# Retention attention and a Strassen MLP on one core: values, last chunk, scores and sums of neighbouring pairs in one run of small tiles, the last block written by quarters on two queues, and one weight piece finished by halves

## The chip, the cores and the metric

The kernel runs on one core of one Trainium2 chip. The metric is the device time of one execution in microseconds (us); times of runs are medians. Nearly all executions here agree within 0.3%, so a change of 0.7% can be seen but a change of 0.1% can not, except inside a trace, where the same stretch repeats within a few hundredths of a microsecond from trace to trace. The granted clock is the share of TensorE's full speed that the chip allowed. All runs on record are of the fast state, with a mean granted clock of 0.995 or more.

## The reference, cut to what matters

```python
# attention, causal with decay: batch 8, heads 8, length 576, head dimension 64
scores = (q @ k.transpose(0, 1, 3, 2)) / 8
Dmat[h, i, j] = gamma[h] ** (i - j) if i >= j else 0
attn = (scores * Dmat) @ v
x = attn.transpose(0, 2, 1, 3).reshape(4608, 512)
# MLP: 4608 tokens, 512 -> 2048 -> 512, PReLU in between
h = x @ w_in
g = max(h, 0) + alpha * min(h, 0)
out = g @ w_out
```

The kernel works the attention in chunks of 64 positions (nine a head): scores inside a chunk, running sums of k-times-v between chunks, and values from both. It takes two heads (a pair) at a time. The MLP runs by blocks of 256 tokens, each in 8 units; from the third block on, a unit is one level of a seven-product Strassen scheme, with weights and inputs combined beforehand. Per unit TensorE computes `ph` (seven products for h), VectorE makes g and its combinations, and TensorE computes `po` (seven products for out).

## The kernel before

In the loop, units of blocks already finished hide the attention of the next batch row. One pair had two separate visits ("excursions") to small array tiles: the scores and sums inside a unit, between its ph and the po of the unit ahead, and the values two units later.

```python
    def mlp_unit(kb, i, front=None):
        ...                                   # 14 matmuls into ph[0], ph[1], 128x128 tiles
        rest = front(ph[0][:, 3]) if front else None   # scores and sums, 64x64 tiles
        ...                                   # ScalarE and VectorE: g from ph
        combine(3, ins)                       # GpSimd: three weight combinations, while some wait
        if rest:
            rest()                            # VectorE: masks of the scores
        pend.append((kb, i, g))
        if len(pend) > 1:
            mlp_out()                         # po of the unit before
...
    def pair_values(n, vn, mt):
        ...
        pv = [ps_tile([P, (j1, NJ - j1)[i], C], f"pv{i}_{n}") for i in range(2)]
        for j in range(NJ):
            for h2 in range(2):               # 128x64 tiles
                nc.tensor.matmul(pv[j >= j1][half(h2), j - (j1 if j >= j1 else 0)],
                                 vn[:, h2, j], mt[:, h2, j], start=True, stop=True)
        ...                                   # ScalarE copies pv into xb, the MLP's input
...
        for u in range(nq):
            front = None
            if u in begin:
                ...
                front = pair_front(n, *turned.pop(n), loaded[n][0], loaded[n][3])
            pop_units(1, front)
            if u - 1 in begin:
                later.pop(0)()                # VectorE: running sums
            if u - 2 in begin:
                n = begin[u - 2]
                if n + 1 < len(pairs):
                    scale_pair(n + 1)         # GpSimd scales q
                    turned[n + 1] = transposes(n + 1)   # VectorE turns k and q
                pair_values(n, loaded[n][3], mts.pop(n))
                del loaded[n]
```

At the end of a block `out_block` adds the products on VectorE, and both halves (128 tokens of 512 values, 256 KB each) leave by SyncE's queue. At the start, `piece_out` turns a raw piece of w_in into the form that TensorE reads: three steps on VectorE, one on GpSimd.

## Time and profile before

| | before |
|---|---|
| time, median (three runs) | 1019.35 us (1018.71 to 1019.44) |
| span in the trace | 1018.5 us |
| TensorE (PE) / VectorE (DVE) / ScalarE (ACT) / GpSimd (POOL) busy | 98 / 76 / 26 / 18% |
| first Strassen unit begins | 153.95 us |
| from there to the ninth unit's start | 57.06 us |
| ninth unit's start to the last unit's start (119 units, 22 pairs) | 793.02 us |
| last matmul's end to the end of the span | 5.11 us |

The last four rows are read from the timeline of PE: a unit begins with the first record of its ph group. They cut the span into the parts that the change touches. The page's fourth part gives the shares of the chain that ended last, that is, of the work followed back from the last instruction, at each step to what released it; in the kernel before:

```profile
PE 94%; DVE 3%; DMA 1%; ACT 0%; issue 0%; SPq 0%; POOL 0%; DVEq 0%; ACTq 0%
```

The 3% of DVE are the one long stretch in which PE is not the chain; it lies in the loop's first 50 us.

### The profile page before, as it was taken

To read this page: it belongs to the slowest core of one execution; us is meant where nothing else is said; L and a number is where in the kernel's file an instruction comes from. 1 tells how busy PE (TensorE), PEld (TensorE's weight loads), DVE (VectorE), ACT (ScalarE), POOL (GpSimd) and SP (SyncE) were. 2 spreads that over 40 slices of the span, in tenths; PEclk is the share of its full clock that TensorE was granted. 3 is DMA by queue.
4 is the path that set the end of the run, shared out by engine and by line. 5 is a ranking of instruction groups with operands and counts; after the bars stand their busy time and mean duration, and the time that the engine had idled before them with its cause. 6 is when DMAs were issued, how large, how long until landed. Compare 5 with 4: busy or idle time off the path is not lost.

```text
span 1018.5 us, 23084 instructions
## 1 busy us (share of the span) xinstructions
PE 1001.3 (98%) x9385; PEld 894.2 (88%) x9385; DVE 778.3 (76%) x2086; ACT 269.4 (26%) x605; POOL 179.2 (18%) x201
## 2 busy tenths in 40 slices
PE   6999999999999999999999999999999999999997
PEld 5666668899999999999999999999999999999997
DVE  6669966878887888768778788887878777667665
ACT  4556653223222222122021312232222211000000
POOL 5656674300100020100010000200020001010000
PEclk8999999999999999999999999999999999999999
DMA  9975744322231323112112313222313000000000
GB/s 238 238 194 140 185 74 103 60 60 48 52 64 40 63 37 69 25 45 48 44 25 56 60 45 60 57 48 54 62 45 60 13 23 1 22 1 21 2 21 22
DMA packets 229308, 64.30 MB, mean 63 GB/s; under 512 B 214337, under 2 KB 222545, under 8 KB 229201
## 3 DMA queue, kind: packets, MB, share of 16 engines
q1 hardware_dynamic: 227088, 62.29, 27.1%
q8 instruction: 74, 1.21, 0.5%
q10 hardware_dynamic: 2112, 0.53, 0.3%
q14 instruction: 34, 0.27, 0.1%
HBM read 53.35 MB, written 9.44 MB: 62 GB/s over the span
## 4 chain that ended last, share of the span: by engine, by line
PE 94%; DVE 3%; DMA 1%; ACT 0%; issue 0%; SPq 0%; POOL 0%; DVEq 0%; ACTq 0%
PE ph L463 38%; PE po L381 37%; PE ph L419 6%; PE po L398 6%; PE pv L656 3%; PE ps L614 1%; PE ps L620 1%; DMA w_out<-in_k_dram 1%; PE ph L614 1%; DVE su L589 0%; DVE g L476 0%; PE pt L697 0%; DVE mt L636 0%; PE ps L716 0%; PE ps L556 0%
## 5 line engine op out<-in xcount | busy, mean ns | idle before, releaser
L381 PE MATMUL po<-w_out,g 128*128 128x256 f32 x1792 | 410.9, 381 | 0.2
L381 PEld LDWEIGHTS po<-w_out,g 128*128 128x128 f32 x1792 | 330.1, 190 | 42.7 <-DVE g L487 1.3
L476 DVE TENSOR_TENSOR g<-ph,g 128x256 f32<-128x256 f32 (+1 forms) x512 | 187.0, 386 | 127.2 <-ACT g L471 75.2
L463 PE MATMUL ph<-xb,w_in 128*128 128x128 f32 x2048 | 272.7, 276 | 0.0
L463 PEld LDWEIGHTS ph<-xb,w_in 128*128 128x128 f32 x2048 | 257.1, 192 | 7.9 <-issue 0.7
L463 PE MATMUL ph<-xt,w_in 128*128 128x128 f32 x1536 | 213.8, 275 | 0.7 <-DVE g L476 0.7
L463 PEld LDWEIGHTS ph<-xt,w_in 128*128 128x128 f32 x1536 | 192.2, 192 | 1.1 <-PE ph L463 0.8
L487 DVE TENSOR_TENSOR g<-g 128x128 f32<-128x128 f32 x512 | 127.2, 289 | 5.4
L471 ACT COPY g<-ph 128x128 f32<-128x128 f32 x128 | 34.1, 266 | 327.7 <-PE ph L463 217.1
L528 POOL TENSOR_TENSOR qx<-qx,tabx 128x576 f32<-128x576 f32 x28 | 32.3, 1153 | 379.6 <-DMA qx<-in_q_dram 223.4
L481 DVE SCALAR_TENSOR_TENSOR g<-g 128x512 f32<-128x512 f32 x128 | 91.3, 714 | 3.8
L479 DVE TENSOR_SCALAR g<-g,alpha 128x256 f32<-128x256 f32 x256 | 84.3, 370 | 2.8
L597 ACT COPY vn<-su 64x512 f32<-64x512 f32 x56 | 34.6, 617 | 135.2 <-DVE su L591 134.5
L419 PE MATMUL ph<-xb,w_in 128*128 128x256 f32 x256 | 61.7, 397 | 0.8 <-POOL w_in L314 0.8
L419 PEld LDWEIGHTS ph<-xb,w_in 128*128 128x128 f32 x256 | 50.1, 198 | 11.0 <-issue 2.4
L398 PE MATMUL po<-w_out,g 128*128 128x512 f32 x128 | 58.6, 599 | 0.9 <-DVE g L435 0.9
L625 DVE SCALAR_TENSOR_TENSOR mt<-ph,th,mask 64x64 f32<-64x64 f32 x48 | 13.6, 283 | 52.5 <-PE ph L614 52.2
L665 ACT COPY xb<-pv 128x256 f32<-128x256 f32 (+3 forms) x84 | 22.7, 321 | 109.8 <-PE pv L656 109.8
L636 DVE SCALAR_TENSOR_TENSOR mt<-ps,th,mask 64x256 f32<-64x256 f32 x96 | 46.1, 481 | 2.3
L533 ACT ACTIVATE vn<-vn,tabv 64x576 f32<-64x576 f32 x56 | 43.3, 774 | 8.7 <-DMA vn<-in_v_dram 7.8
L398 PEld LDWEIGHTS po<-w_out,g 128*128 128x128 f32 x128 | 23.4, 190 | 24.5 <-issue 22.9
L589 DVE SCALAR_TENSOR_TENSOR su<-su,gch 128x64 f32<-128x64 f32 x84 | 43.1, 513 | 2.1
(134 smaller groups left out, 717.0 us busy)
## 6 DMA issues: line engine op xcount, KB each, us to landing
out_dram<-osb SPq DMA_DIRECT2D x36, 256.0 KB, 2.3
kx<-in_k_dram SPq DMA_DIRECT2D x112, 72.0 KB, 2.6
qx<-in_q_dram SPq DMA_DIRECT2D x112, 72.0 KB, 3.0
vn<-in_v_dram SPq DMA_DIRECT2D x56, 144.0 KB, 3.2
kn<-in_k_dram SPq DMA_DIRECT2D x56, 144.0 KB, 3.3
raw<-in_moe_w_in_dram SPq DMA_DIRECT2D x24, 256.0 KB, 4.5
raw<-in_moe_w_out_dram SPq DMA_DIRECT2D x10, 512.0 KB, 5.4
w_in<-in_moe_w_out_dram SPq DMA_DIRECT2D x6, 512.0 KB, 5.7
```

Source lines behind the costliest of these rows:

```text
L381: nc.tensor.matmul(acc[kb][n // 2][:, n % 2, :], g[:, x, :], w_out[i][:, y, :], start=(i == 0 and n % 2 == 0), stop=(i == NU - 1 and (n % ...
L398: nc.tensor.matmul(acc[kb][m], g[:, 2 * x + m], w_out[i][:, 2 * x:2 * x + 2].rearrange("p x f -> p (x f)"), start=(i == 0 and x == 0), sto ...
L419: nc.tensor.matmul(ph[:, x], w_in[i // UST][:, cc // 2 * 2 + x, i % UST, cc % 2], xb[kb][:, cc], start=(cc == 0 and x == 0), stop=(cc == N ...
L463: nc.tensor.matmul(ph[m][:, o], w_in[i // UST][:, l, i % UST, cc], r[:, cc], start=(n in (0, 3) and cc == 0), stop=(n in (2, 6) and cc == ...
L476: nc.vector.tensor_tensor(out=o, in0=x0, in1=x1, op=ALU.add)
L479: nc.vector.tensor_scalar(g[:, 4 + 2 * m:6 + 2 * m], g[:, 2 * m:2 * m + 2], 0.0, alpha[:, fc:fc + 1], ALU.min, ALU.mult)
L481: nc.vector.scalar_tensor_tensor(out=g[:, 0:4].rearrange("p x t -> p (x t)"), in0=g[:, 0:4].rearrange("p x t -> p (x t)"), scalar=0.0, in1 ...
L487: ins = nc.vector.tensor_tensor(out=g[:, o, :], in0=g[:, x0, :], in1=g[:, x1, :], op=op)
L533: nc.scalar.activation(vn[x, h2], vn[x, h2], ACTF.Copy, scale=tabv[x, c:c + 1])
L589: nc.vector.scalar_tensor_tensor(out=su[:, j], in0=su[:, j - 2], scalar=g2, in1=su[:, j], op0=ALU.mult, op1=ALU.add)
L597: nc.scalar.copy(vn[half(h2), h2, 1:], su[half(h2)])
L636: nc.vector.scalar_tensor_tensor(out=mt[to, h2, p2:NJ - 1:2], in0=ps[p2][half(x), 0], scalar=th[to, 3, h:h + 1], in1=mask[to, None, :].to_ ...
```

## The change

The intent is to enter and leave the small tiles once a pair instead of twice: after the po of one unit come the values of pair n-1, then the last chunk's scores of pair n, then its other scores and sums, then the next unit's ph. The values now use the two ph banks, which are empty at that moment, and the last chunk's scores take the free corner of the second. Apart from that, the last block leaves in four quarters on two queues, and the second piece of w_in is finished in halves. The diff, cut to its core:

```diff
@@ piece_out
+            for f in (slice(0, P), slice(P, HM)) if at == 1 else (slice(0, HM),):
+                dst_e, c_e, a_e, hi_e, lo_e = [y[:, :, f] for y in (dst, c, a, hi, lo)]
                 ...                          # the same three VectorE steps and GpSimd step
@@ out_block
+        if kb == NKB - 1:
+            for (m, x), eng in (((0, 0), nc.sync), ((1, 1), nc.scalar), ((0, 1), nc.sync),
+                                ((1, 0), nc.scalar)):
+                t0 = kb * TB + m * P
+                eng.dma_start(out[t0:t0 + P, x * HM:(x + 1) * HM], osb[:, m, x])
+            return
@@ mlp_unit
-        rest = front(ph[0][:, 3]) if front else None
-        if rest:
-            rest()
@@ the loop
+    def joint(n):
+        pv = [ps_h.tile([P, 8, C], FP32, tag=f"psh{m}", name=f"pv{m}_{n}") for m in range(2)]
+        extra = pv[1][:, 7]
+        def last_chunk():
+            if n < len(pairs):
+                kT, qT = turned[n]
+                for h2 in range(2):
+                    nc.tensor.matmul(extra[half(1 - h2)], kT[half(h2), chunk(NJ - 1)],
+                                     qT[half(h2), chunk(NJ - 1)], start=True, stop=True)
+        if n - 1 in mts:
+            pair_values(n - 1, loaded.pop(n - 1)[3], mts.pop(n - 1), pv, last_chunk)
+        else:
+            last_chunk()
+        if n == len(pairs):
+            return
+        pair_front(n, *turned.pop(n), loaded[n][0], loaded[n][3], extra)
+        ...                                   # load_pair(n + 1), operands(n + 1) later
-        (positions of pairs and the loop shown above)
+        at = [u + (u % NU == 0) for u in (c * nq // NPAIR + 2 for c in range(NPAIR))]
+        if b == 2:
+            at = [0, 3] + at[1:]
+        for u in range(nq):
+            first = queue[0][1] == 0
+            pop_units(1)
+            if later and not first:
+                later.pop(0)()
+            if u in at:
+                joint(n)
+                n += 1
```

More of the change, by code (lines that the diff above doesn't have):

```diff
@@ L306, in piece_out @@
             c = ps_h.tile([P, 2, HM], INT32, tag="psh1", name=f"wc_{at}")
-            nc.vector.tensor_scalar(c.bitcast(FP32), a, HI_MIN, HI_MAX, ALU.max, ALU.min)
-            nc.vector.tensor_scalar(c, c, 3, 0x3FFFFFF8,
-                                    ALU.logical_shift_left, ALU.bitwise_and)
-            nc.vector.scalar_tensor_tensor(out=dst.bitcast(INT32), in0=hi, scalar=-0x40000000,
-                                           in1=c, op0=ALU.bitwise_and, op1=ALU.bitwise_or)
-            nc.gpsimd.tensor_tensor(out=dst.bitcast(INT32), in0=dst.bitcast(INT32), in1=lo,
-                                    op=ALU.add)
+            for f in (slice(0, P), slice(P, HM)) if at == 1 else (slice(0, HM),):
+                dst_e, c_e, a_e, hi_e, lo_e = [y[:, :, f] for y in (dst, c, a, hi, lo)]
+                nc.vector.tensor_scalar(c_e.bitcast(FP32), a_e, HI_MIN, HI_MAX, ALU.max, ALU.min)
+                nc.vector.tensor_scalar(c_e, c_e, 3, 0x3FFFFFF8,
+                                        ALU.logical_shift_left, ALU.bitwise_and)
+                nc.vector.scalar_tensor_tensor(out=dst_e.bitcast(INT32), in0=hi_e,
+                                               scalar=-0x40000000, in1=c_e,
+                                               op0=ALU.bitwise_and, op1=ALU.bitwise_or)
+                nc.gpsimd.tensor_tensor(out=dst_e.bitcast(INT32), in0=dst_e.bitcast(INT32),
+                                        in1=lo_e, op=ALU.add)
             free.append(t)
@@ L449, in combine_x, with mlp_unit @@
             nc.gpsimd.tensor_tensor(out=o, in0=x0, in1=x1, op=ALU.subtract)
-    def mlp_unit(kb, i, front=None):
+    def mlp_unit(kb, i):
         if kb not in xt:
@@ L508, in enqueue, with pop_units @@
                 queue.extend((kb, i) for i in range(NU))
-    def pop_units(n, front=None):
+    def pop_units(n):
         for _ in range(min(n, len(queue))):
             kb, i = queue.pop(0)
-            mlp_unit(kb, i, front)
+            mlp_unit(kb, i)
             if i == NU // 2 and kb + 1 < NKB and ready[kb + 1] <= done[0]:
@@ L601, with pair_front @@
     later = []
-    def pair_front(n, kT, qT, kn, vn):
+    def pair_front(n, kT, qT, kn, vn, extra):
         c = pairs[n][1]
@@ L607, in pair_front @@
         assert C == D and NJ == 9
-        def products(extra):
-            ps = [ps_tile([P, 2, NM - 1, C], f"ps{p2}_{n}") for p2 in range(2)]
-            for j in (NJ - 1, *range(NJ - 1)):
-                for h2 in range(2):
-                    x = half((1 - h2, h2)[j % 2])
-                    nc.tensor.matmul(extra[x, 0:C] if j == NJ - 1 else ps[j % 2][x, 0, j // 2],
-                                     kT[half(h2), chunk(j)], qT[half(h2), chunk(j)],
-                                     start=True, stop=True, skip_group_check=True)
-            for j in range(NJ - 1):
-                for h2 in range(2):
-                    x = half((h2, 1 - h2)[j % 2])
-                    nc.tensor.matmul(ps[j % 2][x, 1, j // 2], kn[half(1 - h2), j],
-                                     vn[half(1 - h2), h2, j], start=True, stop=True,
-                                     skip_group_check=True)
-            for h2 in range(2):
-                to = half(1 - h2)
+        ps = [ps_tile([P, 2, NM - 1, C], f"ps{p2}_{n}") for p2 in range(2)]
@@ new lines, in pair_front @@
+        for j in range(NJ - 1):
+            for h2 in range(2):
+                x = half((1 - h2, h2)[j % 2])
+                nc.tensor.matmul(ps[j % 2][x, 0, j // 2],
+                                 kT[half(h2), chunk(j)], qT[half(h2), chunk(j)],
+                                 start=True, stop=True, skip_group_check=True)
+        for j in range(NJ - 1):
+            for h2 in range(2):
+                x = half((h2, 1 - h2)[j % 2])
+                nc.tensor.matmul(ps[j % 2][x, 1, j // 2], kn[half(1 - h2), j],
+                                 vn[half(1 - h2), h2, j], start=True, stop=True,
+                                 skip_group_check=True)
@@ new lines, in pair_front @@
+        for h2 in range(2):
+            nc.scalar.copy(mt[half(h2), h2].rearrange("p j s -> p (j s)"), qT[half(h2)])
+        for h2 in range(2):
+            to = half(1 - h2)
+            nc.vector.scalar_tensor_tensor(
+                out=mt[to, h2, NJ - 1], in0=extra[to],
+                scalar=th[to, 3, 2 * c + h2:2 * c + h2 + 1], in1=mask[to],
+                op0=ALU.mult, op1=ALU.mult)
+        for p2 in range(2):
+            for h2 in range(2):
+                h, to, x = 2 * c + h2, half(1 - h2), (1 - h2, h2)[p2]
@@ L625, in products @@
                 nc.vector.scalar_tensor_tensor(
-                    out=mt[to, h2, NJ - 1], in0=extra[to, 0:C],
-                    scalar=th[to, 3, 2 * c + h2:2 * c + h2 + 1], in1=mask[to],
+                    out=mt[to, h2, p2:NJ - 1:2], in0=ps[p2][half(x), 0],
+                    scalar=th[to, 3, h:h + 1],
+                    in1=mask[to, None, :].to_broadcast([C, NM - 1, C]),
                     op0=ALU.mult, op1=ALU.mult)
-            def rest():
-                for h2 in range(2):
-                    nc.scalar.copy(mt[half(h2), h2].rearrange("p j s -> p (j s)"), qT[half(h2)])
-                for p2 in range(2):
-                    for h2 in range(2):
-                        h, to, x = 2 * c + h2, half(1 - h2), (1 - h2, h2)[p2]
-                        nc.vector.scalar_tensor_tensor(
-                            out=mt[to, h2, p2:NJ - 1:2], in0=ps[p2][half(x), 0],
-                            scalar=th[to, 3, h:h + 1],
-                            in1=mask[to, None, :].to_broadcast([C, NM - 1, C]),
-                            op0=ALU.mult, op1=ALU.mult)
-                later.append(lambda: pair_sums(vn, running_sums(n, ps[0][:, 1], ps[1][:, 1])))
@@ L643, in products, with pair_values @@
-            return rest
-        return products
-    def pair_values(n, vn, mt):
+        later.append(lambda: pair_sums(vn, running_sums(n, ps[0][:, 1], ps[1][:, 1])))
+    def pair_values(n, vn, mt, pv=None, then=None):
         b, c = pairs[n]
@@ L652, in pair_values @@
         j1 += w if NJ - j1 > 6 else 0
-        pv = [ps_tile([P, (j1, NJ - j1)[i], C], f"pv{i}_{n}") for i in range(2)]
+        pv = pv or [ps_tile([P, (j1, NJ - j1)[i], C], f"pv{i}_{n}") for i in range(2)]
         for j in range(NJ):
@@ L657, in pair_values @@
                                  vn[:, h2, j], mt[:, h2, j], start=True, stop=True)
+        if then:
+            then()
         j = 0
@@ L945, with operands @@
     enqueue(1)
-    for b in range(2, B):
-        nq, first, at = len(queue), b * NPAIR, {}
-        for c in range(NPAIR):
-            u = c * nq // NPAIR
-            while queue[u][1] in (0, NU - 1):
-                u += 1
-            assert u + 2 < nq and (not at or at[c - 1] + 2 < u)
-            at[c] = u
-        begin = {u: first + c for c, u in at.items()}
-        for u in range(nq):
-            front = None
-            if u in begin:
-                n = begin[u]
-                if n + 1 < len(pairs) and n + 1 not in loaded:
-                    loaded[n + 1] = load_pair(n + 1)
-                front = pair_front(n, *turned.pop(n), loaded[n][0], loaded[n][3])
-            pop_units(1, front)
-            if u - 1 in begin:
-                later.pop(0)()
-            if u - 2 in begin:
-                n = begin[u - 2]
-                if n + 1 < len(pairs):
-                    scale_pair(n + 1)
-                    turned[n + 1] = transposes(n + 1)
-                pair_values(n, loaded[n][3], mts.pop(n))
-                del loaded[n]
+    def operands(n):
+        scale_pair(n)
+        turned[n] = transposes(n)
@@ new lines, in joint @@
+    def joint(n):
[4 more added lines that the diff above has]
+                kT, qT = turned[n]
+                for h2 in range(2):
+                    nc.tensor.matmul(extra[half(1 - h2)], kT[half(h2), chunk(NJ - 1)],
[7 more added lines that the diff above has]
+        pair_front(n, *turned.pop(n), loaded[n][0], loaded[n][3], extra)
+        if n + 1 < len(pairs):
+            if n + 1 not in loaded:
+                loaded[n + 1] = load_pair(n + 1)
+            later.append(lambda: operands(n + 1))
@@ new lines @@
+    mts.clear()
+    n = 2 * NPAIR
+    for b in range(2, B):
+        nq = len(queue)
+        at = [u + (u % NU == 0) for u in (c * nq // NPAIR + 2 for c in range(NPAIR))]
+        if b == 2:
+            at = [0, 3] + at[1:]
+        for u in range(nq):
+            first = queue[0][1] == 0
+            pop_units(1)
+            if later and not first:
+                later.pop(0)()
+            if u in at:
+                assert not later
+                joint(n)
+                n += 1
@@ L975 @@
         enqueue(b)
+    assert n == len(pairs) + 1
     pop_units(len(queue))
```

## The prediction

> **What bounds the kernel now.** I read the page first, then the chain that ended last, then single stretches of the timeline. From the page of the kernel before, busy time and the granted clock:
>
> ```profile
> PE 1001.3 (98%) x9385; PEld 894.2 (88%) x9385; DVE 778.3 (76%) x2086; ACT 269.4 (26%) x605; POOL 179.2 (18%) x201
> ...
> PEclk8999999999999999999999999999999999999999
> ```
>
> TensorE (PE) is busy for 98% of the span, VectorE (DVE) for 76%, ScalarE (ACT) for 26%; the last row shows full clock but for the first slice. The waits view confirms it: apart from the first 60 us no PE wait is longer than 0.7 us. So from about 204 us on, time is the sum of what PE is given, and a change must take PE time away or stop PE from stretching. Next the chain that ended last, 240 to 262 us (start us, length us, what):
>
> ```profile
> 241.68 0.20 PE ph L614 x2
> 241.88 0.03 PE ps L614 x2
> 241.91 0.03 PE ph L614 x2
> 241.94 0.46 PE ps L614 x27
> 242.40 0.47 PE ps L620 x32
> 242.87 3.22 PE po L381 x14
> 246.09 3.12 PE ph L463 x28
> 249.22 3.02 PE po L381 x14
> ...
> 258.39 1.20 PE pv L656 x36
> 259.59 2.43 PE ph L463 x20
> ```
>
> Here PE alone makes the chain. A unit of the second stage is 28 matmul records on ph (3.12) and 14 on po (3.02), together 6.14. One pair of heads adds two excursions into small array tiles: scores and sums (L614, L620, 64x64 tiles) and values (L656, 128x64 tiles). Scores and sums take 0.20+0.03+0.03+0.46+0.47 = 1.19 us, and the po group after them takes 3.22 instead of 3.02: 1.39 in all. Values take 1.20, and the ph group after them 3.32 instead of 3.12: 1.40. The work proper is smaller. Of L620, 32 records in 0.47 is 14.7 ns each, so the 68 records of scores and sums are worth 1.00; the starts of L656 in the trace lie 58.5 ns apart for every two, so its 36 are worth 1.05. The rest, **0.39 and 0.35 us, is the price of going in and out** of small tiles, about 0.15 in and 0.20 out.
>
> [...] It also shows a change between two small modes, in the timeline of PE:
>
> ```profile
> 54.00 0.68 PE L811 MATMUL pv<-w_out,w_out 64*64 64x64 f32 x16
> 54.61 0.65 PE L818 MATMUL pv<-w_out,w_out 64*32 64x64 f32 x32
> ```
>
> L811 is 64x64, L818 is 64x32. The last L811 record starts at 54.00+0.68-0.22 = 54.46 (one lasts 0.218), L818 at 54.61: 0.15 us where the step inside L811 is 0.05. With a slow second step this change costs some 0.12 us, a third of going out and in again.
>
> [...] the ScalarE copy at L583 reads other columns than VectorE's L636 does, and yet waits for it (timeline of ACT):
>
> ```profile
> 352.21 0.27 ACT L471 COPY g<-ph 128x128 f32<-128x128 f32 x1 [1.99 <-DVE mt L625]
> ...
> 355.56 0.37 ACT L583 COPY su<-ps 128x256 f32<-128x256 f32 x1 [1.49 <-DVE mt L636]
> ```
>
> [...] The trace has 0.54 granted from 19.2 to 26.0 us, where the first unit stands. [...]
>
> **The change part by part.** (a) *One excursion.* Before, 24 pairs in the loop made 24 excursions for scores and 24 for values. After, the built order shows 25: values of pair n-1, the last chunk's scores of n, then its other scores and sums, back to back between po of one unit and ph of the next. The first has no values, the last no scores. The matmuls are the same in number and shape. 48-25 = 23 excursions at 0.37 fall away, and 23 inner changes from 128x64 to 64x64 at 0.12 come in: 23 x 0.25 = **-5.7 us**, all of it on PE, thus on the path.
>
> (b) *Where the pieces stand.* Values now go to the two ph banks instead of two of the attention banks. So they must wait until VectorE has emptied ph of the unit just ended, and the next unit's ph must wait until ScalarE has emptied the values. By durations of before, with values starting at T: ph ended at T-3.0 (one po group), and an undisturbed unit has its four L476 done about 1.4 us after ph (1007.0 to 1008.4 at the end of the trace), so there is no wait in front. Behind, from the built order: the first copy of values ends at T+1.2, then a copy of qT into mt (0.67), then the rest of the values (0.37+0.25), end at T+2.75. The last chunk's two masks share that bank, so they wait for all of it: 2 x 0.28, end T+3.4. PE reaches the second ph bank at T+1.05+0.15+0.12+1.0+0.2 (modes, work, way out) and half a ph group, about 1.35: T+3.9. **Hidden, with 0.5 us to spare.** VectorE then does the transpose of the next qT (0.77), four masks (4 x 0.48) and the running sums between the next unit's own steps. From a like sequence of before (351.55 to 363.90, less one unit's 3.6 and 0.4 idle) that is 8.35 us, so the next unit's g is ready at T+11.3; PE wants it at T+11.8. That is also 0.5 us of room. Where GpSimd runs beside it (one running sum, L589, took 1.31 us at 173.0 while GpSimd combined weights, against a mean of 0.51) or a block's output falls in, it may be lost; I take 0.03 us a pair, **+0.7 us**.
>
> (c) *Start of the loop.* In the timeline of PE from 153 to 204 us the ph and po groups are stretched at four places (0.85, 0.35, 0.28, 0.34; 1.8 in sum). As a check, scores of two pairs three units apart lie 22.49 us apart here and 21.23 later, and the next distance is 0.7 too long: 2.0. In the chain this stretch runs over VectorE, after a DMA of q which the queue held behind output of the first stage. In the built order after, that q load stands ahead of the output, its scaling ahead of the next block's combinations, and values come three or four units after their scores instead of two. I expect half of it back: **-1.0 us**.
>
> (d) *Last block by quarters.* Timeline of the end:
>
> ```profile
> 1011.65 0.43 DVE L367 TENSOR_TENSOR osb<-po,s 128x256 f32<-128x256 f32 x1 [0.78 <-ACT s L362]
> ...
> 1013.98 0.41 DVE L368 TENSOR_TENSOR osb<-po,u 128x256 f32<-128x256 f32 x1
> 1014.09 1.08 SPq L371 DMA_DIRECT2D out_dram<-osb  x2
> ```
>
> The first quarter is ready at 1012.08, the last at 1014.39. Before, both halves go out of one queue after 1014.05, the second issued behind the first's 0.5 us, and 512 KB drain at 358 GB/s (the table by stretches) until 1016.4. After, three quarters are on their way by 1014.4; the last is issued at once on ScalarE's queue, lasts 128 KB / 358 GB/s = 0.37 us after the same 0.86 us from issue to first byte, and ends at 1015.7: **-0.7 us**.
>
> (e) *w_in's second piece by halves.* GpSimd ends that piece at 19.17 us. By the build's waits the unit's first matmul needs only the first piece (17.3) and the xb copies (19.11). The second piece is needed after two of four chunks, at half clock 3.4 us later. So the halves gain **0.0**; three more VectorE instructions cost nothing on the path.
>
> Sum: -5.7+0.7-1.0-0.7 = -6.7; 1019.35-6.7 = 1012.7.
>
> **The rivals.** *A new wait eats the saving.* For it: the ph banks now carry values, the masks stand behind all copies, and the two margins in (b) are but 0.5 us; 0.3 us lost in each of 24 joints gives 7 us and the result would be 1019. Against: the margins come from durations of this trace, and before had the same VectorE work per pair without a PE wait after 204 us. *VectorE becomes the bound.* It does some 23 us per four units of 27, and joints are now even (every four units; three at the first two, six or seven in the long block) where before they alternated three and five; that speaks against it, and for up to 1 us more gain. *The inner mode change costs as much as a full one.* Then 23 x 0.02 is left of (a), result about 1018. The 64x64 to 64x32 change speaks against. *The inner change is free:* 23 x 0.37 = 8.5, result about 1010. *The end is hidden anyway:* no, nothing runs beside the last transfer[...].
>
> **Range and chances.** Middle 1012.7. Low end 1009.8: inner change nearly free and all of (c) back. High end 1017.0: 0.2 us lost in most joints, (c) not gained. Two per cent would be 20.4 us, over twice all excursion overhead there is (48 x 0.37 = 17.8, of which the change can reach half); slower by that much would need 0.8 us per joint. So within 2%: 0.98.
>
> **What would show it.** The chain of after should have, once per pair, values, ph's last chunk, scores and sums in a row, about 2.3 to 2.4 us with one stretched ph group (3.32) behind, instead of 1.39 and 1.40 apart. The step from the last values record to the last-chunk record gives the inner change (0.15 expected). (b) is wrong if the waits view has ph waiting for VectorE's masks or ScalarE's copies, or po stretched past 3.2 in the second unit behind a joint. (c): ph and po groups from 153 to 204 us without the stretches. (d): last transfers done 0.7 us sooner after the last matmul. (e): the first unit starts near 19.26 and takes 6.8 us again; if the half-clock window falls elsewhere, up to 3.3 us would come from there and not from the change. The prediction as a whole is wrong if PE's busy sum falls by 5 us and idle or stretched groups grow by as much.

## The result

The changed kernel took 1012.37 us in the median (1010.99 to 1012.88, four runs) against 1019.03 (1018.08 to 1019.44, four runs) of the kernel before in the same rounds. The ratio is 0.9934, 95% interval 0.9917 to 0.9951: within two per cent, as predicted, and 0.3 us from the predicted time. A ratio here is the mean time of one kernel's fast runs over that of the other's fast runs of the same rounds, so it is not quite the ratio of the medians. Two later series of the changed kernel gave 0.9917 and 0.9924; the three ratios are worth 6.7, 8.5 and 7.7 us, 7.6 in the mean.

From the page of the changed kernel, busy time and the shares of the chain that ended last:

```profile
PE 994.0 (98%) x9385; PEld 891.5 (88%) x9385; DVE 770.5 (76%) x2089; ACT 267.2 (26%) x605; POOL 179.1 (18%) x202
...
PE 98%; DMA 1%; issue 0%; DVE 0%; ACT 0%; SPq 0%; DVEq 0%
```

PE's busy sum fell by 7.3 us and the share of DVE in the chain is gone: the chain is PE nearly from end to end. The chain around one pair (start us, length us, what):

```profile
178.96 1.20 PE pv L656 x36
180.16 0.20 PE pv L965 x2
180.36 0.03 PE ps L620 x2
180.38 0.03 PE pv L965 x2
180.42 0.46 PE ps L620 x27
180.88 0.47 PE ps L626 x32
181.35 3.32 PE ph L474 x28
```

This is the merged run: values (1.20), then the last chunk, scores and sums (0.20+0.03+0.03+0.46+0.47 = 1.19), then one stretched ph group (3.32 instead of 3.12). Together 2.59 us beyond the plain groups, where before it was 1.39+1.40 = 2.79. **The lengths of values and of scores are exactly what they were; the one thing that went is one slow group, 0.20 us.** ("Slow" is a group of 128x128 matmuls beside small tiles; its matmuls are the same, and it takes 0.20 us more in the chain.) The waits view has one line to look at (engine and line, what for, total, times, longest):

```profile
DVE mt L633 <- ACT xb L667: 39.7, 22, 1.9
```

VectorE's masks of the last chunk do wait for the copies of the values, as the prediction's (b) said. But PE waits for nothing in the whole loop: it is busy for all of the 940 us from 60 to 1000.

The end of the changed kernel, from the timeline:

```profile
1004.09 2.31 SPq L378 DMA_DIRECT2D out_dram<-osb  x2
...
1005.75 1.02 ACTq L378 DMA_DIRECT2D out_dram<-osb  x2
1005.97 0.41 DVE L372 TENSOR_TENSOR osb<-po,u 128x256 f32<-128x256 f32 x1
```

The last quarter is done at 1006.38 and lands at 1008.27, 1.89 us later; before, the last half was done at 1014.39 and landed at 1017.36, 2.97 us later. From the last matmul to the end of the span it is 3.89 us instead of 5.11.

The parts of the span, from the timelines, for this and the experiments below (us; the ratio is to the kernel before of the same rounds):

| run | first Strassen unit at | first to ninth unit | ninth to last | last matmul to end | median | ratio |
|---|---|---|---|---|---|---|
| before | 153.95 | 57.06 | 793.02 | 5.11 | 1019.03 | 1 |
| changed | 152.40 | 56.17 | 787.45 | 3.89 | 1012.37 | 0.9934 |
| changed, second series | 151.48 | 56.17 | 787.46 | 3.90 | 1010.54 | 0.9917 |
| changed, third series | 153.21 | 56.17 | 787.45 | 3.91 | 1011.54 | 0.9924 |
| e1_tail | 153.00 | 57.05 | 793.16 | 3.89 | 1018.15 | 0.9992 |
| e2_halves | 153.85 | 57.05 | 793.32 | 5.25 | 1019.54 | 1.0011 |
| e3_merge | 152.14 | 56.20 | 787.46 | 5.10 | 1012.59 | 0.9945 |
| e4_split | 152.69 | 58.25 | 792.70 | 3.90 | 1018.59 | 1.0002 |
| e5_inner | 151.61 | 57.40 | 800.34 | 3.88 | 1025.71 | 1.0064 |
| e6_warm | 151.72 | 56.18 | 787.45 | 3.89 | 1010.94 | 0.9926 |
| e7_nocomb (wrong result) | 153.92 | 55.17 | 793.24 | 5.09 | 1017.49 | 0.9987 |
| e8_warm4 | 153.59 | 56.17 | 787.45 | 3.90 | 1012.28 | 0.9928 |
| e10_order | 153.16 | 56.18 | 787.45 | 3.90 | 1011.76 | 0.9933 |

e9_masks is not in the table, since its ph groups are cut by waits and cannot be counted in the same way. The loop repeats within 0.02 us over traces of the changed kernel. So the spread of the runs (1010.1 to 1012.9 over its three series) belongs almost wholly to the first 150 us, and there to a small part: from the third unit's first ph (at 44.4 to 46.9 us) to the first Strassen unit it is 107.05 us in all fourteen traces, so what differs lies ahead of it. One thing has to be known for comparing columns: the kernels with the new loop (changed, e3 to e6, e8, e10) have one more visit for scores ahead of the ninth unit (three, against two before) and one less behind it, worth 1.39 us. So the ninth to the last unit saves 793.02-1.39-787.45 = 4.18 us, 0.20 for each of the 21 pairs merged there, and the first to the ninth 57.06+1.39-56.17 = 2.28, of which two merged pairs are 0.4 and the stretches 1.9.

### The profile page after: what moved, and what is told of

It is laid out like the page before. It is cut to its first block, busy times and chain, and to the rows that moved or that the text cites. A ratio compares the mean times of both kernels' runs of the same rounds, so it can differ in the third digit from the quotient of the medians.

```text
span 1009.2 us, 23132 instructions
## 1 busy us (share of the span) xinstructions
PE 994.0 (98%) x9385; PEld 891.5 (88%) x9385; DVE 770.5 (76%) x2089; ACT 267.2 (26%) x605; POOL 179.1 (18%) x202
## 4 chain that ended last, share of the span: by engine, by line
PE 98%; DMA 1%; issue 0%; DVE 0%; ACT 0%; SPq 0%; DVEq 0%
PE ph L474 40%; PE po L392 38%; PE ph L430 6%; PE po L409 6%; PE pv L656 3%; PE ps L620 1%; PE ps L626 1%; DMA w_out<-in_k_dram 1%; PE pv L965 1%; PE pt L699 0%; PE pv L777 0%; PE ps L563 0%; PE ps L718 0%; PE pu L581 0%; PE pv L766 0%
## 5 line engine op out<-in xcount | busy, mean ns | idle before, releaser
L488 DVE TENSOR_SCALAR g<-g,alpha 128x256 f32<-128x256 f32 x256 | 85.7, 377 | 3.7
L460 POOL TENSOR_TENSOR xt<-xb 128x256 f32<-128x256 f32 x16 | 11.6, 728 | 196.6 <-PE ph L474 196.6
L633 DVE SCALAR_TENSOR_TENSOR mt<-pv,th,mask 64x64 f32<-64x64 f32 x48 | 13.6, 283 | 40.2 <-ACT xb L667 39.7
```

The source lines that it names most:

```text
L488: nc.vector.tensor_scalar(g[:, 4 + 2 * m:6 + 2 * m], g[:, 2 * m:2 * m + 2], 0.0, alpha[:, fc:fc + 1], ALU.min, ALU.mult)
```

## The experiments

My theory after the two traces was a sum of independent terms: one way in and out saved in each of 23 pairs (4.6 us), the stretches at the loop's start gone (1.9), the end 1.2 shorter, the halves worth nothing, and a first part that differs by chance. The rivals: the halves brought what came sooner in the first part; the loop's gain is another schedule and not the merging; an inner change of tiles costs as much as a full way in and out; the new wait behind the ph banks is no danger in the first place. Twelve runs followed: e1 to e4 in one series on one chip, e5 to e7 with the changed kernel again in a second, e8 and e9 with the changed kernel a third time, and e10 alone.

### One part at a time: e1_tail, e2_halves, e3_merge

e1_tail is the kernel before with only this part of the change:

```diff
+        if kb == NKB - 1:
+            ...   # the four dma_start of the quarters, as in the change
+            return
```

> The kernel before plus the last block by quarters on two queues, nothing else. If the two traces are read rightly, the time from the last matmul to the end of the span falls from 5.1 us to 3.9 us and the whole by 1.2 us. The prediction's working says 0.7 us. If the gain of the end were chance (the transfers hidden or as slow in quarters), the end stays at 5.1 us and the whole within 0.3 us of before.

The end is 3.89 us as in the changed kernel; the runs give 0.9992 (0.9980 to 1.0004), 0.8 us with an interval that holds both 0 and 1.2. The trace settles it: **the quarters are worth 1.2 us**, since the four traces that lack them have 5.09 to 5.25 and every one that has them 3.88 to 3.91.

e2_halves is the kernel before with only the loop over halves in `piece_out`:

```diff
+            for f in (slice(0, P), slice(P, HM)) if at == 1 else (slice(0, HM),):
```

> The kernel before plus the second piece of w_in by halves, nothing else. The trace of the changed kernel had its first Strassen unit 1.55 us sooner than before, with 0.82 instead of 0.54 granted clock in the first unit. If that came of the halves, this run is 1 to 1.5 us faster than before and its first unit (ph of 256 columns, 16 records) begins 0.6 us sooner. If it is the place where the half-clock window happened to fall, the mean of the runs is within 0.3 us of before, the first unit begins within 0.3 us of 19.26, and its length varies between about 5 and 7 us from run to run without regard to the kernel.

The ratio is 1.0011 (0.9999 to 1.0023), and the first unit begins at 19.16 instead of 19.26. It takes 5.36 us here, 6.74 before; yet the first Strassen unit begins at 153.85, where it did before. The halves bring nothing, as (e) said; the part before the loop has its own chances, to which I come below.

e3_merge is the changed kernel without the other two parts:

```diff
-            for f in (slice(0, P), slice(P, HM)) if at == 1 else (slice(0, HM),):
-        if kb == NKB - 1:
-            ...   # the quarters
```

> The changed kernel without the quarters at the end and without the halves: one excursion and the new loop alone. By the chain of the two traces a merged pair costs 2.59 us where the two excursions cost 2.79, so 23 x 0.20 = 4.6 us, and the stretches at the start of the loop (2.0 us) are gone: 6.6 us faster than before. If each merged pair saves the predicted 0.25 us and all of the start is back: 7.7. If the inner change cost as much as a full way in and out: about 2.

Its loop is that of the changed kernel to 0.03 us in both columns, its end that of before. The ratio 0.9945 (0.9933 to 0.9958) is worth 5.6 us (4.3 to 6.8); by the trace the loop is 6.4 us shorter.

### Merging or another schedule: e4_split

The loop of the change (positions, loads, order of VectorE's work, values in the ph banks), but scores go back between ph and po of a unit. It was built from the changed kernel and so has the quarters and halves too; the text on record calls it "the run above with its loop kept", which leaves that out, and its time has to be compared with the changed kernel's. The scheduler had at first pulled one of the scores in behind the values; a scheduling dependence on the unit's last ph matmul, without a semaphore, keeps the two visits apart. The scheduler also moved the first of the seven po products (two of the 14 records) from behind the scores to directly behind the values, which the text on record does not have.

```diff
-            pair_values(n - 1, ..., pv, last_chunk)
-        pair_front(n, *turned.pop(n), loaded[n][0], loaded[n][3], extra)
+            pair_values(n - 1, ..., pv)
+        front = pair_front(n, *turned.pop(n), loaded[n][0], loaded[n][3])   # run inside mlp_unit
```

> The run above with its loop kept (same positions of the pairs, same order of loads and of VectorE's work, values in the ph banks), but with two excursions again: the values ahead of a unit, the last chunk, scores and sums between its ph and po as before. If the saving of the merged excursion is the way in and out alone, this is slower than the run above by 4.6 us (0.20 a pair; 5.7 if the prediction's 0.25 is right) and faster than before by 2.0 us, with ph and po groups from 153 to 204 us without stretches. If the stretches came of the two excursions and not of the place of the pairs, they are back and it is within 0.5 us of before.

Half of this held. From the ninth unit to the last it takes 792.70, that is 5.25 more than the changed kernel. The waits view tells what of it is not the visit:

```profile
PE po L392 <- DVE g L491: 2.3, 4, 1.0
```

Four waits of po for VectorE's g make 2.3 us. The two longest (1.0 and 0.56) lie ahead of the ninth unit; the two behind it make their visits 0.46 us longer each. 5.25 less 0.92 is 4.33, over 21 pairs **0.206 us a pair: merging is what saves it**, with the rest of the new loop in place but for one moved po product (above).

The other half failed in the number: the ratio is 1.0002, not 2 us below before, and first to ninth unit takes 58.25, hardly less than the 57.06+1.39 = 58.45 that the kernel before would take with the same visits. But no ph or po group there is stretched. What is lost is the two waits, at the po product that was moved (PE's and VectorE's timeline):

```profile
175.29 0.70 PE L392 MATMUL po<-w_out,g 128*128 128x256 f32 x2 [0.99 <-DVE g L491]
```

```profile
171.81 2.71 DVE L489 TENSOR_SCALAR g<-g,alpha 128x256 f32<-128x256 f32 x2
```

In its place behind the scores it would want g some 4.4 us later, when that was ready (176.3 us). The two waits make their visits 1.69 us longer, and 58.25-1.69 = 56.56 is what the changed kernel's 56.17 comes to with two pairs unmerged. So e4_split does not show that the merging takes the stretches away; it rather speaks for the new positions, but a run with this product in its place was not made. Why VectorE was late here (2.71 us for two steps that take 0.61 elsewhere) is the subject of e7.

### The price of an inner change: e5_inner

The same matmuls, in six runs instead of two a pair: values of three chunks, last chunk, three, scores, three, sums.

```diff
-            pair_values(n - 1, loaded.pop(n - 1)[3], mts.pop(n - 1), pv, last_chunk)
+            pair_values(n - 1, loaded.pop(n - 1)[3], mts.pop(n - 1), pv,
+                        {2: last_chunk, 5: scores, 8: products})   # behind these chunks
```

> The changed kernel with the merged excursion cut into six runs instead of two: values of three chunks, the last chunk's scores, values of three, the other scores, values of three, the sums. That is five inner changes of tile shape a pair instead of one, with the same matmuls: 4 x 23 = 92 more. If an inner change costs 0.20 us, as the step into the scores did in the traces of both kernels, the whole is 18 us slower than the changed kernel (about 1030.5); with the 0.12 of the prediction 11 us (about 1023.5); if it costs nothing, the time stays at 1012.4.

It came out between the two numbers: 1025.71, 14 us above the changed kernel's 1011.5 (mean of its three medians). Chain of e5_inner around one pair:

```profile
178.17 0.50 PE pv L665 x12
178.67 0.26 PE pv L974 x4
178.93 0.50 PE pv L665 x12
179.43 0.62 PE ps L620 x32
180.06 0.50 PE pv L665 x12
180.56 0.62 PE ps L628 x32
181.18 3.32 PE ph L474 x28
```

3.01 us from the first values to ph, against 2.39 in the changed kernel: 0.62 more for four more changes, **0.15 us each**. Over the loop it is the same: 800.34-787.45 = 12.89, over 21 pairs and four changes 0.153. The single records say where it goes: inside a run the values' pairs start 0.058 us apart; at a change one step is 0.158, and the step after it 0.106, so 0.10+0.05 = 0.15.

This also corrects how I had read the step into the last chunk (0.20) in both kernels, and with it the prediction's price of the scores' visit. Its work was taken as 68 records at 14.7 ns, 1.00 us. But the four tiles run their own records side by side (the first records of all four start within 0.04 us), and the two that serve the even chunks have 18 of the 68 each: 18 steps of 0.058 are 1.04. Then scores and sums of 1.19 hold 1.04 of work and one change of 0.15, like the values (18 pairs at 0.058, 1.04, and 0.15).

### Order inside the tiles: e10_order

Before I had seen that, I suspected a loss in the order, because the last chunk and chunk 0 use the same two tiles one after the other.

```diff
-        for j in range(NJ - 1):
+        for j in (1, 0, 3, 2, 5, 4, 7, 6):
```

> The changed kernel with the chunks of the scores and of the sums taken in the order 1, 0, 3, 2, 5, 4, 7, 6 instead of 0 to 7; the last chunk stays first. In the trace of the changed kernel the last chunk and chunk 0 use the same two of the four tiles one after the other, and the records of the other two tiles begin a step later. If that is why scores and sums take 1.19 us where 68 records in fours at 0.058 us and one change of shape at 0.15 us make 1.14, each pair saves 0.05 us: the loop from the ninth unit to its last falls from 787.46 (the same within 0.02 in five traces) to 786.4, and the whole by 1.2 us. If the 0.05 belongs to the change of shape itself, the loop stays at 787.46. The medians of the runs vary by 1 us and can hardly tell; the loop's length in the trace can.

A miss: 787.45 again. The chain of e10_order shows the first records closer together:

```profile
180.92 0.20 PE pv L965 x2
181.13 0.01 PE ps L620 x2
181.14 0.04 PE pv L965 x2
```

The second pair of tiles now follows after 0.01 us where it was 0.03, yet from the first of these records to the next ph group it is 1.19 us in the timeline of every pair, as in the changed kernel. So the length fits the count, by which the two tiles with 18 records set it whatever the order. The run's ratio, 0.9933 (0.9919 to 0.9946), says nothing else.

### What stretched the loop's start: e7_nocomb

The prediction read the stretches there as a q load held behind output. The second theory is that GpSimd's last weight combinations slow VectorE's work for the pair. e7_nocomb is the kernel before with these twelve combinations replaced by nine plain copies on ScalarE. Its result is wrong on purpose (relative error 0.81).

```diff
-        combine(3, ins)
+        for _ in range(min(3, len(waiting))):
+            wt, (o, y0, y1, op) = waiting.pop(0)
+            if o != 1:
+                cp = nc.scalar.copy(wt[:, o], wt[:, y0])      # behind ins, as before
```

> The kernel before with GpSimd's twelve weight combinations in the first four units of the loop taken away (ScalarE writes nine plain copies in their place, so the results are wrong on purpose). If the stretched ph and po groups of 153 to 204 us come of VectorE's steps running slow beside GpSimd (its running sums took 0.85 and more instead of 0.29 there), the stretch of 1.8 us shrinks to 0.6 us or less and the whole is 1.2 to 1.8 us faster than before. If they come of the q load behind the first stage's output, as the prediction read it, the stretch stays and the time is within 0.5 us of before.

First to ninth unit takes 55.17 instead of 57.06: 1.89 us, the whole stretch. Runs: 0.9987 (0.9979 to 0.9996), twelve of them, 1.3 us. VectorE's and GpSimd's timelines of the kernel before at that place:

```profile
172.51 1.84 DVE L589 SCALAR_TENSOR_TENSOR su<-su,gch 128x64 f32<-128x64 f32 x2
...
174.61 1.09 DVE L589 SCALAR_TENSOR_TENSOR su<-su,gch 128x64 f32<-128x64 f32 x1
```

```profile
171.66 3.96 POOL L324 TENSOR_TENSOR w_in<-w_in 128x512 f32<-128x512 f32 x3 [4.78 <-DVE g L487]
```

And VectorE's in e7_nocomb, where GpSimd has nothing in this window:

```profile
172.49 0.61 DVE L594 SCALAR_TENSOR_TENSOR su<-su,gch 128x64 f32<-128x64 f32 x2
...
173.35 0.28 DVE L594 SCALAR_TENSOR_TENSOR su<-su,gch 128x64 f32<-128x64 f32 x1
```

Three running sums (128x64) took 1.84+1.09 us beside GpSimd's 3.96 us of combinations, and 0.61+0.28 without. The q load had nothing to do with it: the queue issues it at 161.71 in e7_nocomb and at 161.73 before, and VectorE turns q at 165.39 and 165.41; both stand where they stood, and the stretch is gone. In the changed kernel the same combinations still slow VectorE (two steps of L488 at 172.02 took 2.71 us, 0.61 elsewhere), but the pair's masks and sums are done by 168.2, since they begin at once behind the joint, and PE does not notice; that this is why is read from the trace and was not tried apart. Each of the three slow instructions reads two SBUF tensors, and the trace ties their ends to GpSimd's: they end at 173.00, 174.35 and 175.70, each 0.07 or 0.08 us after one of GpSimd's three combinations ends (172.93, 174.27, 175.62), while a sum with one input in PSUM took its usual 0.48 us at 172.00, within the first of them. But the slowed L488 and e4_split's L489 read one tensor only. Why these ends fall together is not shown here.

### The margin behind the ph banks: e9_masks

In the changed kernel the last chunk's masks, which hold the second ph bank, stand first among VectorE's masks. They end at 181.92 in the pair shown, and PE's first record for that bank starts at 182.72: 0.8 us of room. e9_masks puts them last (with scheduling dependences, no semaphore).

```diff
-        (last chunk's two masks) ; (four masks of the other scores)
+        (four masks of the other scores) ; (last chunk's two masks)
```

> The changed kernel with VectorE's two masks of the last chunk, which hold the second ph bank, put behind the transpose of q and the other four masks instead of ahead of them; nothing else is moved. In the changed kernel these two end 2.96 us after the values begin and TensorE comes to the second ph bank after 3.93 us, so the bank is free 1.0 us early. Put last they end after about 5.8 us: TensorE should wait some 1.6 to 1.9 us in the ph group of each of 24 joints, 38 to 45 us in all, result 1050 to 1057. If the wait behind the ph banks were no danger in the first place (the rival that the prediction gave 0.7 us to), the time stays within 5 us of the changed kernel's.

The median is 1048.64, ratio 1.029 (1.0275 to 1.0304), 37 us above the changed kernel in the same rounds (1011.54). PE's largest wait, and VectorE and PE around one joint (two timelines):

```profile
PE ph L474 <- DVE mt L641: 30.1, 22, 1.5
```

```profile
184.15 1.99 DVE L634 SCALAR_TENSOR_TENSOR mt<-ps,th,mask 64x256 f32<-64x256 f32 x4
186.16 0.58 DVE L641 SCALAR_TENSOR_TENSOR mt<-pv,th,mask 64x64 f32<-64x64 f32 x2
```

```profile
183.99 1.46 PE L392 MATMUL po<-w_out,g 128*128 128x256 f32 x6
186.89 0.68 PE L474 MATMUL ph<-xt,w_in 128*128 128x128 f32 x4 [1.43 <-DVE mt L641]
```

The wait is 1.4 us in each pair, a little less than the 1.6 expected, and the time a little under the expected range. "Nothing else is moved" does not hold for TensorE: the scheduler drew the six po records shown ahead of the rest of ph, which fill a part of what would else be waiting. So the wait that the prediction gave 0.7 us to is real and worth about five times the whole saving; **it stays hidden because these two masks go first**. Of the 37 us the listed waits explain 30; but from one joint to the next, four units on, it is 28.87 us (231.74 to 260.61) where the changed kernel has 27.18, so 1.69 a pair, and 22 such pairs make 37. The list counts idle time from the modelled end of a matmul, which in an unbroken group lies 0.16 us behind the start of the next one.

### The first 150 us: e6_warm, e8_warm4 and the changed kernel again

The traces of the first unit (16 ph records of 256 columns) differed: 6.74 us before, 5.17 changed, 6.62, 5.36, 3.69, 5.38 in e1 to e4. e6_warm puts idle matmuls into the gaps ahead of it (six and four), e8_warm4 only the four directly ahead:

```diff
+    def warm(n):
+        t = ps_h.tile([P, P], FP32, tag="psh0", name=f"warm_{n}")
+        for _ in range(n):
+            nc.tensor.matmul(t, ident, ident, start=True, stop=True)
+    warm(4)
     plain_unit(0, 0)
```

> The changed kernel with ten matmuls of the identity by itself, whose results nobody reads, in the two gaps of TensorE before the first unit (six ahead of the values' second part, four ahead of the unit). If the 3 us by which the first unit's length varies from trace to trace (6.74, 5.17, 6.62, 5.36, 3.69, 5.38 in six traces) come of a half-clock window that idle time before the unit brings on, the first unit takes 3.4 to 3.7 us here at a granted clock of 0.95 or more, the runs lie within 1.5 us of each other, and their median is 1 to 2 us below that of the changed kernel. If the window comes anyway, or what follows waits for loads instead, the median is within 0.5 us of the changed kernel's.

> The changed kernel once more, for the spread of its runs and a second trace beside the runs above. 1012.4 us within 1 us; the loop from its ninth unit to its last takes 787.5 us as in the first trace, within 0.2; where the runs differ, the first 150 us differ.

> The changed kernel with four matmuls of the identity by itself ahead of the first unit only, in the 0.77 us in which TensorE waits for the xb copies. The run with ten had the first unit at full clock (3.69 us) but began it 1.7 us later[...]. If four are enough to keep the clock up and delay nothing, the first unit begins at 18.5 to 19.0 and takes 3.7 us, and the median is 1 to 1.5 us below the changed kernel's of the same rounds. If the half-clock window is set by the longer gap ahead of it (1.3 to 2.2 us), the first unit takes 5 to 7 us as before in some of the runs and the medians agree within 0.5 us.

> The changed kernel a third time, as the measure for the two runs above on the same chip: 1010 to 1012.5 us, the loop from the ninth unit to the last 787.5 us.

The changed kernel again gave 1010.54 and 1011.54: the first is almost 2 us below the 1012.4 expected, the loop is the same to 0.01 us in both, so the difference lies ahead of it. For the idle matmuls the clock part came as expected: both have the first unit at full clock (3.69 us). But e3_merge, e5_inner and e10_order have it too (3.69) without any, so that the idle matmuls did it is not shown. The time part did not come. e6_warm gives 1010.94 against 1010.54 of the changed kernel beside it, e8_warm4 1012.28 against 1011.54; neither is told apart from it, and the runs lie no closer together (1010.1 to 1013.0 and 1009.3 to 1013.2). In e6_warm the first unit begins 1.8 us later (20.30 instead of 18.46): the six matmuls stand ahead of the values' second part, most of which runs from 17.54 instead of 16.33. In e8_warm4 the half clock came elsewhere. PE's timeline there:

```profile
19.09 3.69 PE L430 MATMUL ph<-xb,w_in 128*128 128x256 f32 x16
...
40.60 5.40 PE L409 MATMUL po<-w_out,g 128*128 128x512 f32 x8
```

and busy times with the granted clock (third from the end) in two stretches of it:

```profile
19.00:22.00 3.00, 2.91 (x14) 2.60 (x15) 2.86 (x7) 2.96 (x6) 1.83 (x3) 1.00 0.87 199
...
40.00:43.00 3.00, 2.79 (x7) 1.41 (x8) 0.58 (x1) 2.73 (x7) 2.97 (x4) 0.62 0.95 316
```

The po group of 8 records takes 5.40 us at 40.60, where the changed kernel's second trace has 3.70. Read in steps of 1 us from 14 to 60 us, the granted clock is 0.50 in every full step of such a stretch of half clock and 1.00 outside it. Summed over these steps, the clock lost is 0, 1.7 or 3.4 us in each of the 13 traces up to e9, so no, one or two windows of 3.4 us at half rate, beginning at 17 to 19 us in most and at 41 us in e8_warm4. What brings one on is not shown: in the 3.4 us ahead of the half clock PE was busy for 1.37 us in the kernel before and for 1.84 in e8_warm4, while in e5_inner, which lost none, it was busy for 1.65 of the 3 us from 16 to 19. In the traces without idle matmuls PE also stood still for 1.3 to 2.7 us from about 15 us on ("issue" in the timelines: 1.33 in the changed kernel's second trace, 2.66 in e7_nocomb). In ten traces that I looked at it went on 1.2 to 1.4 us after a transfer of the instruction queue had ended; that is seen side by side only, not tested. I take the spread of the runs to be these windows and the waits around them, as an estimate; that each microsecond is explained is not shown, since the first Strassen unit begins between 151.5 and 154.0 and does not simply follow the windows lost (e3_merge lost none and began it at 152.14).

**No version run here beats the changed kernel** by more than the spread. One idea was not run: values in 64x64 tiles would need no inner change (0.15 a pair by e5_inner).

## Why the prediction was right or wrong

The predicted 1012.7 lies beside the measured 1012.37; over three series the gain is 7.6 us where 6.7 was predicted. By its terms (the measured ones from the traces):

| term | predicted | measured | by |
|---|---|---|---|
| (a) one visit instead of two | -5.7 | -4.6 (23 x 0.20) | chain; e4_split 0.206 a pair |
| (b) new waits at the ph banks | +0.7 | 0 | waits view |
| (c) start of the loop | -1.0 | -1.9 | first to ninth unit, less the visits |
| (d) quarters | -0.7 | -1.2 | end; e1_tail |
| (e) halves | 0.0 | 0 | e2_halves |
| sum | -6.7 | -7.7 | |

(a) The mechanism held: the same matmuls, and one way in and out less a pair. The size did not: 23 x (0.37-0.12) was mis-sized in both factors of the difference. A visit costs 0.10 into the slow group ahead, 0.15 inside and 0.10 in the group behind (by the starts around the merged run shown, po ahead takes 3.12 instead of 3.02 and ph behind 3.23 instead of 3.13), 0.35 on the mean, not 0.37, because the scores' work is 1.04 and not 1.00. The inner change costs 0.15, not 0.12: taking it from one step between 64x64 and 64x32 tiles missed the second slow step (0.05). The difference is 0.20, not 0.25. That the trace shows the step into the scores as long as ever (0.20) does not make the rival "as dear as a full one" true: such a change would have left 0.02 a pair.

(b) The waiting chain was read rightly (masks behind copies, PE behind masks) and with about the right room, 0.8 us where 0.5 was worked out. The 0.03 us a pair charged for it was caution and did not come.

(c) The size was half of what came, and the step that named the cause was wrong: "which the queue held behind output of the first stage". The chain passed through that load, but the load had arrived when it was needed; what made the chain long was the running sums beside GpSimd. The prediction had that very number in hand (one running sum of 1.31 us beside GpSimd) and used it for (b). It also read the first stretch a little short: by the lengths of the groups the four are 0.92, 0.35, 0.28 and 0.35, 1.9 in sum.

(d) The step "512 KB drain at 358 GB/s until 1016.4" was too quick: by the packet records of the trace the two halves took from 1014.92 to 1016.88, 1.96 us or 267 GB/s. Before, the last transfer landed at 1017.36, 2.97 us behind the last sum; the last quarter's packets ended at 1007.92, and it landed 1.89 us behind its sum. The landing came only 0.48 us behind the last packet before and 0.35 in the changed kernel. What of the 1.1 us comes from the second queue and what from the smaller last piece was not tried apart; in the traces the last transfer was issued 0.44 us behind the last sum before and 0.03 after, and landed 2.53 and 1.86 us after its issue, so 0.4 us is the earlier issue and 0.7 the transfer.

(e) held as worked out. Its warning that the half-clock window may fall elsewhere was the right one too: 1.55 of the 9.2 us between the two traces' spans lie in the first 47 us, where of the change only the halves act, and no run shows that they come of the change.

So the total came out close because two terms that were too small and one that was charged for nothing made up for the one that was too large. That is luck, and so is a distance of 0.3 us from the median: the three series of the same kernel differ by almost 2.

## What to carry to other kernels

Price a visit to small tiles by its borders: time the groups ahead and behind as well (0.10 us each here), and count the work by the tile with the most records, not by all records (18 of 68 fit the 1.19 us here). When two such visits were merged here, what was saved was one way in and one way out (0.35) less the change between the two shapes (0.15), and the order of the evictions behind the shared bank decided whether it stayed saved (37 us lost in e9_masks). And before blaming the transfer that a chain of waits passes through, look at whether the engine behind it was running at its usual speed (three running sums took 2.93 us beside GpSimd here and 0.89 without).
